# Decode attention: scores by row matmuls at tile positions, transposed back into the softmax layout, with two more key tiles on PE

## The chip, the cores and the metric

The kernel runs on one core of one Trainium2 chip. The metric is the device time of one launch in microseconds (us). Ratios are the mean time of one kernel's fast runs over that of the other's in the same rounds, so they are not quite the ratios of the medians quoted beside them.

Engines in the profile: PE is the matmul engine, PEld its weight loads, DVE is VectorE, ACT is ScalarE, SPq is the queue of SyncE, which issues the loads.

## The reference

Two independent attention blocks, A and B, one decode step each. Both have batch 8, 32 heads, 4096 cached keys of 128 elements, in bf16. The output is the two results side by side.

```python
def block(x, k_cache, v_cache, wq, wo):          # x [8,1,1024]; caches [8,32,4096,128]
    q = (x @ wq) -> [8, 32, 1, 128]
    scores = einsum("bhqd,bhkd->bhqk", q, k_cache) * 128 ** -0.5
    p = softmax(scores, axis=-1)
    o = einsum("bhqk,bhkd->bhqd", p, v_cache)
    return o.reshape(8, 1, 4096) @ wo
```

There is one query per batch and head, so every cached element is used once. The caches are 1074 of the 1107 MB that are read.

## The kernel before

A *unit* is one (block, head, batch) triple: 1 MB of K and 1 MB of V. There are 512 units, in groups of four. K arrives with 32 tiles of 128x128 per unit (partition = key, free = element). The scores of a unit are made by two engines:

- PE takes the first 12 tiles (`PEJOBS = (4, 2)` counts pairs). It transposes pairs as f32, ACT copies the result to `kt`, and each transposed tile becomes the *stationary* operand of a matmul with the query as a narrow moving operand. The scores land directly in the layout `S` (partition = key).
- VectorE takes the other 20 tiles with one multiply-and-accumulate call (a *dot*) per tile. The trace shows each dot as two instructions, SCALAR_TENSOR_TENSOR and DVE_READ_ACCUMULATOR (10240 of each), so one dot less per unit is 1024 instructions less.

```python
PEJOBS = (4, 2)                       # NPT = 12 tiles on PE, ND = 20 on VectorE
NK = 5; NV = 6                        # slots for K and V loads

def make_SC(q):                       # scores on PE, column layout
    for il in range(PEJOBS[c]):
        for e in range(2):
            pe.matmul(grp[:, gb, col:col + NMOV],                 # NMOV = 32
                      kt[:, ktslot, i * 256 + e:(i + 1) * 256:2], # stationary: 128x128
                      qm[:, blk, qo:qo + NMOV], start=(e == 0), stop=(e == 1))

def make_dots(U):                     # scores on VectorE, one call per tile
    for t in range(ND):
        v.scalar_tensor_tensor(out=junk[:, n % JR, :], in0=knat[:, slot, j*128:(j+1)*128],
            scalar=1.0, in1=qbc_sb[:, U % NQB, :], op0=ALU.mult, op1=ALU.mult,
            accum_out=S_all[:, r, gi * NT + j:gi * NT + j + 1])

def sp_k(U):                          # a K slot is reused when PE and VectorE are done with it
    deps = [("Tpe", Up * NC + NC - 1), ("dot", Up, ND - 1)]       # Up = U - NK
    sp.dma_start(knat[:, slot, :], K[b, h])                       # 128 rows of 8 KB
# ... softmax chain per group, PV matmuls, output projection: not touched in what matters here
```

Of the kernel before, what the change touches and what calls it, by code (L numbers as in the profile page):

```python
# [12 lines left out]
G = 4  # L13
# [5 lines left out]
NR = 3  # L19
NGB = 2  # L20
NOB = 2
NO = 2
NWO = 4
QHJ = 4
NMOV = 32
PEJOBS = (4, 2)
NQB = 8
# [21 lines left out]
def bass_concat_heads__mha_block_cached__mha_block_cached__decode_kernel(  # L49
# [42 lines left out]
    assert H % QHE == 0 and QHE * 128 <= 512  # L92
    NQJ = H // QHE
    PVD = G + 2 + (int(DOTLAG + 0.999) if NDC > 0 else 0)
    DV = PVD - 2
    NV8 = NT // 4
    assert LAG < 4 and NT % 4 == 0 and G == 4
    assert G * NPT + NMOV <= 192 and NMOV <= 64

# [3 lines left out]
    L_OFF = 328  # L103
    QW = 4 * UPB + NMOV

# [7 lines left out]
    with ExitStack() as es:  # L113
# [6 lines left out]
        kt = sb("kt", [128, NKT, NPT * 128], BF16)  # L120
        wq_sb = sb("wq_sb", [128, DC, H * 128], BF16)
        wo_sb = sb("wo_sb", [128, NWO, DO], BF16)
# [8 lines left out]
        junk = sb("junk", [128, JR, 128], BF16)  # L131
        S_all = sb("S_all", [128, NR, G * NT], F32)
        qm = sb("qm", [128, NBLK, QW], BF16)
        P_sb = sb("P_sb", [128, NR, G * NT], BF16)
# [13 lines left out]

        stage = ps("stage", [128, 4, 512], F32)
        grp = ps("grp", [128, NGB, 512], F32)  # L150
# [5 lines left out]
        sem_names += ["xd%d" % i for i in range(NBLK)]  # L156
        sem_names += ["wqd%d" % i for i in range(NBLK)] + ["wqd0a"]
        sem_names += ["kd%d" % i for i in range(NK)]
# [33 lines left out]
        def new_job(pe_ev, ev_ev):  # L192
            jid = len(jobs)
            jobs.append((pe_ev, ev_ev))
            deps = [jobs[jid - 4][1]] if jid >= 4 else []
            return jid % 4, deps

# [25 lines left out]
        def make_Q1(qj):  # L223
            blk, jl = qj // NQJ, qj % NQJ
            h0 = jl * QHE
            pe_ev, ev_ev = ("Q1pe", qj), ("Q1ev", qj)
            bank, sdeps = new_job(pe_ev, ev_ev)

            def emit_pe(pe):
                last = None  # L230
                for c in range(DC):
                    last = pe.matmul(stage[0:Bsz, bank, 0:QHE * 128],  # L232
                                     xT_sb[:, blk, c, :],
                                     wq_sb[:, c, h0 * 128:(h0 + QHE) * 128],
                                     start=(c == 0), stop=(c == DC - 1))
                return last
            wdep = ("wqd0a",) if qj == 0 else ("wqd", blk)
            pe_add(_Op("Q1_%d" % qj, "pe", emit_pe, deps=[wdep, ("Xev", blk)] + sdeps,
                       event=pe_ev, sem="pe_stA"))

            def emit_ev(a):
                return a.copy(qrow[0:Bsz, qj % 3, :], stage[0:Bsz, bank, 0:QHE * 128])
            d2 = [pe_ev]
            if qj >= 3:
                d2.append(("Q2pe", qj - 3))
                pj = qj - 3
                ulast = (pj // NQJ) * UPB + ((pj % NQJ) + 1) * QHE * Bsz - 1
                if ND > 0:
                    d2.append(("QBpe", ulast))
            add(_Op("Q1ev%d" % qj, "act", emit_ev, deps=d2, event=ev_ev, sem="ev_A"))  # L250
# [80 lines left out]
        def make_T(q):  # L331
# [24 lines left out]
            if U - NKT >= 0:  # L356
                d2.append(("SC", (U - NKT) * NC + c))
            if use_act:
# [3 lines left out]

        def make_SC(q):
            U, c = q // NC, q % NC
            blk, h, b = unit_info(U)
            ul = U % UPB
            g = U // G
            gi = U % G
            gb = g % NGB
            ktslot = U % NKT  # L370

            def emit_pe(pe):
                last = None
                for il in range(PEJOBS[c]):
                    i = POFF[c] + il
                    col = S_OFF + gi * NPT + 2 * i
                    for e in range(2):
                        qo = (ul * 2 + e) * 2
                        last = pe.matmul(grp[:, gb, col:col + NMOV],  # L379
                                         kt[:, ktslot, i * 256 + e:(i + 1) * 256:2],  # L380
                                         qm[:, blk, qo:qo + NMOV],
                                         start=(e == 0), stop=(e == 1))
                return last
            deps = [("Tev", q)]
            if gi == 0 and c == 0 and g - NGB >= 0:
                deps.append(("rl", g - NGB))
            if c == 0:
                hl = min(H - 1, (ul * 4 + 2 + NMOV - 1) // (4 * Bsz))
                deps.append(("Q2ev", blk * NQJ + h // QHE))
                deps.append(("Q2ev", blk * NQJ + hl // QHE))  # L390
                deps.append("qmz")
            pe_add(_Op("SC%d" % q, "pe", emit_pe, deps=deps, event=("SC", q), sem="pe_sc"))

        def make_chain_T1(g):
            gb, r = g % NGB, g % NR
            pe_add(_Op("T1_%d" % g, "pe",
                       lambda pe: pe.transpose(grp[0:G, gb, T1_OFF:T1_OFF + 128], pmax[:, r, :], ident_f[:, :]),  # L397
                       deps=[("rmax", g)], event=("T1", g), sem="pe_misc"))

# [114 lines left out]
        def make_chain_rest(g):  # L514
            gb, r, ob = g % NGB, g % NR, g % NOB
            lastq = (g * G + G - 1) * NC + NC - 1
            s_view = S_all[:, r, :]
            d0 = [("SC", lastq)]
            if g - NR >= 0:
                d0.append(("xs", g - NR))  # L520
            add(_Op("copyS%d" % g, "dve",
                    lambda v: v.tensor_copy(  # L522
                        S_all[:, r, :].rearrange("p (g j) -> p g j", g=G)[:, :, 0:NPT],
                        grp[:, gb, S_OFF:S_OFF + G * NPT].rearrange("p (g j) -> p g j", g=G)),
                    deps=d0, event=("copyS", g), sem="dve_misc"))
            d1 = [("copyS", g)]
            if ND > 0:
# [41 lines left out]

        add(_Op("o4z", "dve", lambda v: v.memset(o4[:, :, :], 0.0), event="o4z", sem="dve_misc"))  # L570

        def make_fin(blk):
# [12 lines left out]
        for g in range(NG):  # L585
            ulast = g * G + G - 1
            u_sc = ulast + (NC - 1 + LAG + 1) / float(NC)
            u_dots = ulast + 1 + DOTLAG if ND > 0 else 0.0
            u0 = max(u_sc, u_dots)
# [25 lines left out]
        for hh in range(NHH):  # L615
# [3 lines left out]
            if hh % H == H - 1:  # L619
                at_tick(t + 2, "F", hh // H)  # L620
        last_tick = max(extras.keys())
        order_rank = {"Q1": 0, "Q2": 1, "QB": 2, "T1": 3, "B": 4, "L": 5, "PV": 6, "O": 7, "OP": 8, "F": 9}
        makers = {"T1": make_chain_T1, "B": make_chain_B, "L": make_chain_L, "PV": make_PV,
                  "O": make_O, "Q1": make_Q1, "Q2": make_Q2, "OP": make_OP, "F": make_F, "QB": make_QB}

# [4 lines left out]
        for t in range(0, max(last_tick, NQCH + LAG) + 1):  # L630
            if t < NQCH:
                make_T(t)
            if 0 <= t - LAG < NQCH:
                make_SC(t - LAG)
            for kind, arg in sorted(extras.get(t, []), key=lambda ka: (order_rank[ka[0]], ka[1])):
# [16 lines left out]

        def sp_wq(blk):
            if blk == 0:
                def emit_a(sp):
                    src = blocks[0][3].rearrange("(p c) n -> p c n", c=DC)[:, :, 0:QHE * 128]
                    return sp.dma_start(wq_sb[:, :, 0:QHE * 128], src)
                add(_Op("wq0a", "sp", emit_a, deps=[], event=("wqd0a",), sem="wqd0a", amount=16))
                return

            def emit(sp):
                src = blocks[blk][3].rearrange("(p c) n -> p (c n)", c=DC)
                return sp.dma_start(wq_sb[:, :, :].rearrange("p c n -> p (c n)"), src)
            deps = [("Q1pe", blk * NQJ - 1)]
            add(_Op("wq%d" % blk, "sp", emit, deps=deps, event=("wqd", blk), sem="wqd%d" % blk, amount=16))

        def sp_wq0b():
            def emit_b(sp):
                src = blocks[0][3].rearrange("(p c) n -> p c n", c=DC)[:, :, QHE * 128:H * 128]
                return sp.dma_start(wq_sb[:, :, QHE * 128:H * 128], src)  # L670
            add(_Op("wq0b", "sp", emit_b, deps=[], event=("wqd", 0), sem="wqd0", amount=16))

# [38 lines left out]
        for i in range(NU + DV + 1):  # L711
            if i < NU:
                if i == 2 and NQJ > 1:
                    sp_wq0b()
                for blk in range(1, NBLK):
                    if i == max(3, min(blk * UPB - 40, (blk - 1) * UPB + (NQJ - 1) * QHE * Bsz - 24 + 6)):
                        sp_wq(blk)
                if i % Bsz == 2:
                    sp_wo(i // Bsz)
                sp_k(i)  # L720
# [149 lines left out]
```

## Time and profile before

The median is 2823.28 us over 12 runs (2819.29 to 2825.72).

| | before |
|---|---|
| DMA | 1111 MB, mean 394 GB/s |
| VectorE busy | 2425 us (86%) |
| PE busy | 2185 us (77%) |
| ACT busy | 675 us (24%) |

From the page of the kernel before: the span, the engines' busy time (and number of instructions), the rate in 40 equal slices, and the DMA queues (packets, MB, share of 16 engines' span).

```profile
span 2820.1 us, 60232 instructions
...
PE 2184.9 (77%) x15904; PEld 1214.3 (43%) x15904; DVE 2425.7 (86%) x21829; ACT 675.2 (24%) x1843; POOL 4.9 (0%) x11
...
GB/s 392 420 411 394 394 400 394 395 396 403 401 385 399 398 387 419 394 392 391 398 404 394 387 400 391 396 393 398 396 401 392 397 399 396 396 402 389 396 399 272
DMA packets 159302, 1111.27 MB, mean 394 GB/s; under 512 B 17488, under 2 KB 18512, under 8 KB 27760
...
q1 hardware_dynamic: 158928, 1107.40, 97.7%
q8 instruction: 127, 2.08, 0.3%
q14 instruction: 215, 1.76, 0.2%
...
```

The DMA engines look full (97.7%), but they don't run at one rate: one slice shows 420 GB/s, most show 390 to 400. The windows view of the kernel before (the last three columns are granted PE clock, DMA share, GB/s) shows it more sharply:

```profile
core 0: us, PE busy (x) PEld busy (x) DVE busy (x) ACT busy (x) POOL busy (x), PEclk, DMA share, GB/s
126.00:132.00 6.00, 3.60 (x29) 1.84 (x27) 5.90 (x55) 1.03 (x3) 0.00 (x0) 1.00 1.02 419
1524.00:1530.00 6.00, 4.34 (x41) 2.40 (x39) 5.56 (x52) 1.61 (x6) 0.00 (x0) 1.00 0.95 345
1554.00:1560.00 6.00, 4.14 (x34) 2.27 (x31) 5.93 (x54) 1.04 (x3) 0.00 (x0) 1.00 0.95 356
...
```

Early in the run the rate is 419 GB/s with VectorE 98% busy; later, with VectorE 93 to 99% busy, it falls to 345 and 356 in places. The waits of the load queue, and PE's waits for K (the columns after the colon are us in total, times, longest):

```profile
...
SPq L813 <- DVE junk L322: 2178.7, 507, 16.9
SPq L704 <- PE o L424: 118.0, 103, 6.6
...
```

```profile
...
PE stage L342 <- DMA knat<-in_A_k_cache_dram: 264.3, 154, 20.8
...
PE stage L342 <- DMA knat<-in_B_k_cache_dram: 241.7, 157, 3.2
...
```

It would be natural to read the first of these lines as "VectorE is the bottleneck": 2179 us long the queue waited for a dot to free a K slot. But PE waits 506 us for K, and a K load, once issued, takes 15.4 us to land, six times the 2.6 us that one MB needs at 400 GB/s. Loads are always queued. Something in the DMA, not the issue, is late.

The completion records of the trace tell what. Each load adds 16 to its semaphore. The Trainium skill, "DMA: Bandwidth & Descriptors", § Why a DMA increments its semaphore by 16 and not by 1, says that a DMA "runs on up to 16 SDMA engines that finish independently", each adding one; the trace agrees in that 16 separate increments are recorded for each load. Below are the times of the 16 increments of five K loads, in us after the first of them (computed from the trace's records, not a view of the profile):

```
unit  10:   0.0   0.0   0.1   0.1   0.2   0.2   0.5   1.0   1.5   1.7   1.9   2.0   2.3   2.9   3.0   3.7
unit  20:   0.0   0.0   0.0   0.1   0.1   0.2   1.0   1.1   1.5   1.9   2.0   2.9   3.0   3.3   3.8   6.7
unit  30:   0.0   0.1   0.2   0.2   0.7   1.0   1.1   1.6   1.9   2.0   2.9   3.0   3.0   3.3   3.8  10.5
unit 100:   0.0   0.0   0.0   0.1   0.1   0.1   0.2   0.3   0.3   0.4   0.5   0.8   1.4   1.6   2.8  10.1
unit 300:   0.0   0.2   0.2   0.4   0.4   0.5   0.5   0.5   0.6   0.6   1.0   1.1   1.2   1.3   2.0   9.6
```

One engine falls behind in the first 200 us until it is about 10 us late. There the five K slots stop the others: the first increment of a K load comes a median 5.4 us after its issue, the last 15.4 us. The fifteen are soon done with what is queued, the late one never is. It alone sets the pace from then on.

Two more things from the packet records: K loads land 4.97 us apart in the median where no packet of queue 14 ran in between, and 5.93 us apart where one did; and 187 of the 221 such packets of 8 KB are followed, 0.31 us after their start, by a data packet of 8 KB that took far longer than the usual 309 ns (over 600), in the median 968. After an instant picked at random one finds such a packet in 4% of cases. (The 221 are those of the whole record, the page's 215 those of the span; the times below are from the start of the record, 10.8 us before that of the span.)

```
queue 14 packet at 309.71 us took 333 ns; data packet started 0.32 us after it took 968 ns
queue 14 packet at 327.10 us took 326 ns; data packet started 0.31 us after it took 968 ns
queue 14 packet at 341.29 us took 309 ns; data packet started 0.31 us after it took 839 ns
```

So such a packet costs its engine 0.31 us for itself and 0.968 - 0.309 = 0.66 us by the stretched packet, together 0.97 us. Queues 8 and 14 are of the kind "instruction": 2.08 + 1.76 MB are 64 bytes for each of the 60232 instructions. Queue 8's size fits PE's stream; queue 14's fits the rest, of which VectorE has 22475 instructions (those of the page plus its separate semaphore waits), or 176 packets of 8 KB.

Two groups and a piece of the timeline, for what the change touches. A group's columns are busy us, mean ns of one, idle before; a timeline row is start, us, instruction, count.

```profile
L322 DVE SCALAR_TENSOR_TENSOR junk<-knat,qbc_sb 128x128 bf16<-128x128 bf16 x10240 | 2237.8, 284 | 23.1 <-ACT qbc_sb L299 12.3
...
L322 DVE DVE_READ_ACCUMULATOR junk<-knat,qbc_sb 128x1 f32 x10240 | 826.6, 81 | 0.0
...
L379 PE MATMUL grp<-qm,kt 128*128 128x32 bf16 x6144 | 323.4, 180 | 0.0
...
```

```profile
...
1588.55 0.26 PE L379 MATMUL grp<-qm,kt 128*128 128x32 bf16 x4
1588.74 0.22 PE L291 MATMUL stage<-qrow,sel 8*128 8x128 bf16 x1
1588.89 0.44 PE L342 MATMUL stage<-ident_f,knat 128*128 128x128 f32 x2
1589.17 0.36 PE L379 MATMUL grp<-qm,kt 128*128 128x32 bf16 x8
1589.45 1.89 PE L424 MATMUL o<-vnat,P_sb 128*4 128x512 bf16 x8
...
```

The dots repeat every 0.213 us in the median (from the records). The 12 score matmuls of a unit take 0.19 us plus 0.28 us between the starts of their neighbours. That is 0.47 us per unit.

### The profile page before, as it was taken

To read this page: it belongs to the slowest core of one execution; us is meant where nothing else is said; L and a number is where in the kernel's file an instruction comes from. 1 tells how busy PE (TensorE), PEld (TensorE's weight loads), DVE (VectorE), ACT (ScalarE), POOL (GpSimd) and SP (SyncE) were. 2 spreads that over 40 slices of the span, in tenths; PEclk is the share of its full clock that TensorE was granted. 3 is DMA by queue.
4 is the path that set the end of the run, shared out by engine and by line. 5 is a ranking of instruction groups with operands and counts; after the bars stand their busy time and mean duration, and the time that the engine had idled before them with its cause. 6 is when DMAs were issued, how large, how long until landed. Compare 5 with 4: busy or idle time off the path is not lost.

```text
span 2820.1 us, 60232 instructions
## 1 busy us (share of the span) xinstructions
PE 2184.9 (77%) x15904; PEld 1214.3 (43%) x15904; DVE 2425.7 (86%) x21829; ACT 675.2 (24%) x1843; POOL 4.9 (0%) x11
## 2 busy tenths in 40 slices
PE   5787777778777887678887777877887787787777
PEld 3444444444444444344444444444444444444444
DVE  6888888888888889688888888888888888888886
ACT  2222222222222222122222222222222222222222
POOL 0000000000000000000000000000000000000000
PEclk7888898898988988788898898888888888888888
DMA  9999999999999999999999999999999999999996
GB/s 392 420 411 394 394 400 394 395 396 403 401 385 399 398 387 419 394 392 391 398 404 394 387 400 391 396 393 398 396 401 392 397 399 396 396 402 389 396 399 272
DMA packets 159302, 1111.27 MB, mean 394 GB/s; under 512 B 17488, under 2 KB 18512, under 8 KB 27760
## 3 DMA queue, kind: packets, MB, share of 16 engines
q1 hardware_dynamic: 158928, 1107.40, 97.7%
q8 instruction: 127, 2.08, 0.3%
q14 instruction: 215, 1.76, 0.2%
q10 hardware_dynamic: 32, 0.03, 0.0%
HBM read 1107.33 MB, written 0.03 MB: 393 GB/s over the span
## 4 chain that ended last, share of the span: by engine, by line
DMA 57%; DVE 27%; PE 14%; issue 1%; SPq 0%; ACT 0%; DVEq 0%
DMA knat<-in_B_k_cache_dram 29%; DMA knat<-in_A_k_cache_dram 28%; DVE junk L322 24%; PE o L424 7%; PE stage L342 4%; DVE pmax L530 1%; PE grp L379 1%; PE stage L446 1%; DVE S_all L522 1%; PE grp L403 1%; DVE dg L538 0%; DVE gmax L534 0%; PE stage L232 0%; PE stage L291 0%; PE grp L410 0%
## 5 line engine op out<-in xcount | busy, mean ns | idle before, releaser
L322 DVE SCALAR_TENSOR_TENSOR junk<-knat,qbc_sb 128x128 bf16<-128x128 bf16 x10240 | 2237.8, 284 | 23.1 <-ACT qbc_sb L299 12.3
L424 PE MATMUL o<-vnat,P_sb 128*4 128x512 bf16 x4096 | 1197.2, 446 | 0.0
L342 PE MATMUL stage<-ident_f,knat 128*128 128x128 f32 x3072 | 604.5, 311 | 508.7 <-DMA knat<-in_A_k_cache_dram 264.3
L359 ACT COPY kt<-stage 128x512 f32<-128x512 f32 (+1 forms) x1024 | 495.3, 484 | 1583.5 <-PE stage L342 1578.0
L322 DVE DVE_READ_ACCUMULATOR junk<-knat,qbc_sb 128x1 f32 x10240 | 826.6, 81 | 0.0
L342 PEld LDWEIGHTS stage<-ident_f,knat 128*128 128x128 f32 x3072 | 363.6, 153 | 774.6 <-issue 747.6
L424 PEld LDWEIGHTS o<-vnat,P_sb 128*4 128x4 bf16 x4096 | 342.3, 93 | 558.7 <-issue 259.6
L379 PEld LDWEIGHTS grp<-qm,kt 128*128 128x128 bf16 x6144 | 325.1, 101 | 21.2 <-issue 0.4
L379 PE MATMUL grp<-qm,kt 128*128 128x32 bf16 x6144 | 323.4, 180 | 0.0
L403 PE MATMUL grp<-dg,ones_f 4*128 4x4 f32 x256 | 63.5, 316 | 109.2 <-DVE dg L538 108.6
L454 DVE TENSOR_REDUCE oun<-stage 128x4 f32<-128x16 f32 x128 | 22.4, 175 | 139.6 <-PE stage L446 139.5
L299 ACT CAST qbc_sb<-stage 128x128 bf16<-128x128 f32 x512 | 138.6, 271 | 0.0
L554 ACT ACTIVATE P_sb<-xs_sb 128x128 bf16<-128x128 f32 x128 | 39.6, 309 | 370.7 <-DVE xs_sb L546 370.7
L522 DVE COPY S_all<-grp 128x48 f32<-128x48 f32 x128 | 26.5, 207 | 109.4 <-PE grp L379 109.3
L291 PE MATMUL stage<-qrow,sel 8*128 8x128 bf16 x512 | 119.5, 234 | 0.0
L567 ACT COPY osb<-o 128x512 f32<-128x512 f32 x128 | 74.6, 583 | 151.6 <-PE o L424 151.6
L403 PEld LDWEIGHTS grp<-dg,ones_f 4*128 4x128 f32 x256 | 52.2, 253 | 122.1 <-DVE dg L538 120.3
L446 PE MATMUL stage<-ident_f,osb 128*128 128x128 f32 x512 | 84.4, 288 | 0.7 <-ACT osb L567 0.7
L557 DVE TENSOR_REDUCE l_p<-P_sb 128x4 f32<-128x128 bf16 x128 | 36.6, 286 | 49.8 <-ACT P_sb L554 49.8
L446 PEld LDWEIGHTS stage<-ident_f,osb 128*128 128x128 f32 x512 | 53.9, 141 | 57.9 <-issue 56.8
L534 DVE TENSOR_REDUCE gmax<-grp 4x1 f32<-4x128 f32 x128 | 35.2, 275 | 28.1 <-PE grp L397 27.7
L291 PEld LDWEIGHTS stage<-qrow,sel 8*128 8x128 bf16 x512 | 46.9, 92 | 22.6 <-issue 6.7
(40 smaller groups left out, 441.9 us busy)
## 6 DMA issues: line engine op xcount, KB each, us to landing
knat<-in_A_k_cache_dram SPq DMA_DIRECT2D x256, 1024.0 KB, 15.4
vnat<-in_A_v_cache_dram SPq DMA_DIRECT2D x256, 1024.0 KB, 17.6
knat<-in_B_k_cache_dram SPq DMA_DIRECT2D x256, 1024.0 KB, 15.4
vnat<-in_B_v_cache_dram SPq DMA_DIRECT2D x256, 1024.0 KB, 17.6
wo_sb<-in_A_wo_dram SPq DMA_DIRECT2D x32, 256.0 KB, 18.1
wo_sb<-in_B_wo_dram SPq DMA_DIRECT2D x32, 256.0 KB, 18.1
wq_sb<-in_A_wq_dram SPq DMA_DIRECT2D x1, 7168.0 KB, 28.8
wq_sb<-in_A_wq_dram SPq DMA_DIRECT2D x1, 1024.0 KB, 8.3
```

The source lines that it names most:

```text
L291: return pe.matmul(stage[:, bank, 0:128], sel[0:Bsz, b, :], qrow[0:Bsz, qj % 3, hl * 128:(hl + 1) * 128], start=True, stop=True)
L299: add(_Op("QBev%d" % U, "act", lambda a: a.copy(qbc_sb[:, U % NQB, :], stage[:, bank, 0:128]), deps=d2, event=ev_ev, sem="ev_A"))
L322: return v.scalar_tensor_tensor(out=junk[:, n % JR, :], in0=knat[:, slot, j * 128:(j + 1) * 128], scalar=1.0, in1=qbc_sb[:, U % NQB, :], o ...
L342: last = pe.transpose(stage[:, bank, il * 128:(il + 1) * 128], knat[:, slot, i * 256:(i + 1) * 256].bitcast(F32), ident_f[:, :])
L359: add(_Op("Tev%d" % q, "act", lambda a: a.copy(dst, src), deps=d2, event=ev_ev, sem="ev_A"))
L379: last = pe.matmul(grp[:, gb, col:col + NMOV], kt[:, ktslot, i * 256 + e:(i + 1) * 256:2], qm[:, blk, qo:qo + NMOV], start=(e == 0), stop= ...
L403: lambda pe: pe.matmul(grp[:, gb, B_OFF:B_OFF + G], ones_f[0:G, :], dg[0:G, r, :], start=True, stop=True),
L424: last = pe.matmul(o4[32 * gi:32 * gi + 4, ob, 0:512], P_sb[:, r, gi * NT + 4 * g8:gi * NT + 4 * g8 + 4], vnat[:, slot, g8 * 512:(g8 + 1) ...
L446: last = pe.transpose(stage[:, bank, m * 128:(m + 1) * 128], osb[:, ob, m * 128:(m + 1) * 128], ident_f[:, :])
L522: lambda v: v.tensor_copy(S_all[:, r, :].rearrange("p (g j) -> p g j", g=G)[:, :, 0:NPT], grp[:, gb, S_OFF:S_OFF + G * NPT].rearrange("p ( ...
L554: lambda a: a.activation(out=P_sb[:, r, :], in_=xs_sb[:, r, :], func=ACT_FN.Exp),
L567: lambda a: a.copy(osb[:, ob, :], o4[:, ob, :]),
```

## The change

Scores on PE are turned round: the query (two columns) is the stationary operand, and up to 512 columns of the transposed keys stream past it. Each unit of a group writes its two rows at its own tile position (partitions 0, 32, 64, 96). ACT copies the rows of a group to SBUF, PE transposes them back, and VectorE writes them into `S`. This needs fewer PE instructions and leaves PE room for one more pair of tiles, so VectorE has 18 dots instead of 20 per unit. PSUM is made free by one `grp` bank and one staging bank less, SBUF by loading `wq` in halves.

```diff
-NGB = 2
+NGB = 1
-NMOV = 32
-PEJOBS = (4, 2)
+NSB = 3
+PEJOBS = (4, 3)
 ...
-        wq_sb = sb("wq_sb", [128, DC, H * 128], BF16)
+        wq_sb = sb("wq_sb", [128, DC, HPW * 128], BF16)        # half of the heads at a time
+        srows_sb = sb("srows_sb", [128, 2, 1024], F32)
-        stage = ps("stage", [128, 4, 512], F32)
+        stage = ps("stage", [128, NSB, 512], F32)
+        rows = ps("rows", [128, 2, 512], F32)
 ...
-        def make_SC(q):            # (shown above)
+        def make_SCM(U):
+                for rb, (p0, npair) in enumerate(((0, RB0), (RB0, RB1))):
+                    for e in range(2):
+                        mov = kt[:, ktslot, p0 * 256:(p0 + npair) * 256].rearrange(
+                            "p (i x e) -> p i x e", i=npair, e=2)[:, :, :, e]
+                        last = pe.matmul(rows[32 * gi:32 * gi + 2, rb, 0:npair * 128],
+                                         qm[:, blk, qo:qo + 2], mov,
+                                         start=(e == 0), stop=(e == 1),
+                                         tile_position=(0, 32 * gi))
+        def make_ST(gk):           # transposes back, then VectorE into S_all
+                for il in range(npair):
+                    last = pe.transpose(stage[:, bank, il * 128:(il + 1) * 128],
+                                        srows_sb[:, g % 2, (p0 + il) * 128:(p0 + il + 1) * 128],
+                                        ident_f[:, :])
+                return v.tensor_copy(dst, src)
 ...
-            add(_Op("copyS%d" % g, "dve", ... S_all <- grp ...))
+            add(_Op("srev%d" % g, "act", ... srows_sb <- rows ...))
```

## The prediction

> **What bounds the kernel.** DMA part of the page: 1111.27 MB at a mean of 394 GB/s, yet 6 us stretches (windows view) reach 420 to 425. The trace's completion records show why. Every 1 MB load increments its semaphore 16 times, once per DMA engine. After the first 200 us, fifteen increments come close together, the sixteenth about 10 us later (median spread 9.9). K loads land a median 15.6 us after issue, their first increment after only 4.9: fifteen engines run dry, one never does. K landings are 4.96 us apart (16 packets of 8 KB at 309 ns), or about 5.95 us in every third unit; the extra 1 us falls where a queue-14 packet of 8 KB runs. Queues 8 and 14 are "instruction": 2.08 + 1.76 MB = 64 bytes x 60232 instructions. VectorE has 22475 of them, about 176 packets, one per three units. (The Trainium skill, "Runtime: NRT & Kernel Launch", Instruction fetch mechanics, calls refills mostly hidden; this trace disagrees: each delays its engine about 1 us.) Sum for that engine: 512 x 4.95 + wo 45 + wq 37 + 170 x 0.97 = 2780 us, plus start and tail of about 12 us each, near the 2820 us span. VectorE (86% busy) and PE (77%) keep up; PE waits 506 us in total for K (waits view).
>
> **What the change does.**
> - VectorE: dots per unit 20 to 18, each 0.212 us, so -217 us; the copy of S (128 x 207 ns) becomes 256 evictions (+20 us). Busy near 2230 us. Instructions about 20550, 161 packets.
> - PE: 6144 score matmuls of 32 columns (0.47 us per unit) become 2048 of 512 or 384 columns: an estimated 0.8 us per unit from the 0.225 us repeat of the 512-column PV matmuls (1.5 us if the strided operand costs double); a seventh key transpose (+0.11), seven transposes per group of four (+0.25 per unit). From about 3.7 to 4.4 us of a 5.4 us unit; about 5400 instructions fewer.
> - ACT: bigger second kt copy, one 128x896 copy per group: 675 to about 850 us, off the path.
> - wq in 3 and 4 KB rows instead of 7 and 64 KB: +1 us per engine.
> - Group chain one unit longer, one grp bank, three staging banks: hidden, since the slow engine always has about five loads queued. At the tail +2 us.
>
> **How much counts.** Only VectorE's instruction packets: 15 x 0.97 = -14 us, +1, +2. The 200 us of VectorE work taken away are off the bound.
>
> **Prediction: 2810 us, range 2792 to 2835.** Faster by over 2%: 0.03; within 2%: 0.91; slower by over 2%: 0.06.
>
> **What would show it.** Right: one of 16 increments still about 10 us late; K intervals still 4.96 or about 5.95 us, the long ones a little rarer; queue 14 about 1.63 MB, queue 8 about 1.74; VectorE near 79% busy, its idle time grown by what its work shrank; about 396 GB/s. Wrong: the spread shrinks well under 10 us, so an engine, most likely PE, holds issues back; then PE's waits for K shrink toward zero and waits on the ACT row copy or the staging banks grow.
>
> **What would make it wrong.** Strided 512-column reads at half rate plus drains between tile positions, putting PE above 5.4 us per unit; a staging bank waiting for VectorE's in-order queue; or the lag being due to something other than instruction packets, so that relieving VectorE pays more.

## The result and the profile after

The change is slightly faster: a median of 2803.22 us over 10 runs (2801.73 to 2808.02) against 2823.28 us. The ratio is 0.993 (95% interval 0.9921 to 0.994), or about 20 us.

The page of the changed kernel, the same lines as above:

```profile
span 2801.4 us, 52449 instructions
...
PE 2345.9 (84%) x13216; PEld 1148.2 (41%) x13216; DVE 2242.4 (80%) x19910; ACT 904.6 (32%) x1971; POOL 4.8 (0%) x11
...
GB/s 389 420 405 407 397 395 395 394 411 399 400 400 395 399 403 395 402 400 404 397 392 401 399 403 394 391 412 402 397 401 384 406 407 389 396 401 406 397 388 285
DMA packets 162238, 1110.77 MB, mean 397 GB/s; under 512 B 17520, under 2 KB 18544, under 8 KB 30864
...
q8 instruction: 106, 1.74, 0.2%
q14 instruction: 196, 1.61, 0.1%
...
```

VectorE has 183 us less to do (2425 to 2242 us), and the span fell by 19 us. PE has 17% fewer matmuls but is busier. The rate is 397 GB/s for 394. Queue 14 carries 196 packets for 215, queue 8 carries 106 for 127.

The groups, and PE's timeline:

```profile
L330 DVE SCALAR_TENSOR_TENSOR junk<-knat,qbc_sb 128x128 bf16<-128x128 bf16 x9216 | 2018.1, 285 | 16.7 <-ACT qbc_sb L307 13.0
...
L387 PE MATMUL rows<-kt,qm 128*2 128x512 bf16 (+1 forms) x2048 | 537.7, 388 | 0.0
...
L418 DVE COPY S_all<-stage 128x32 f32<-128x32 f32 (+1 forms) x256 | 47.4, 185 | 181.4 <-PE stage L407 181.4
...
L551 ACT COPY srows_sb<-rows 128x896 f32<-128x896 f32 x128 | 115.9, 905 | 40.8 <-PE rows L387 40.8
...
```

```profile
...
1512.15 0.95 PE L387 MATMUL rows<-kt,qm 128*2 128x512 bf16 x4
1513.04 0.23 PE L299 MATMUL stage<-qrow,sel 8*128 8x128 bf16 x1
...
1513.67 1.89 PE L454 MATMUL o<-vnat,P_sb 128*4 128x512 bf16 x8
...
```

The four score matmuls of a unit now take 0.89 us from their start to that of the next instruction, for 0.47 before. The strided moving operand did not halve the rate: 448 columns on average in about 0.22 us each, much like the 512-column PV matmuls (eight in 1.8 us). The copy of rows on ACT takes 905 ns a group.

The waits of the load queue, and those of the engines that bear on it:

```profile
...
SPq L847 <- DVE junk L330: 1699.1, 426, 7.6
SPq L737 <- PE o L454: 541.8, 150, 13.8
...
```

```profile
...
PE stage L350 <- DMA knat<-in_A_k_cache_dram: 203.2, 144, 12.7
...
PE stage L350 <- DMA knat<-in_B_k_cache_dram: 191.1, 150, 12.7
...
DVE S_all L418 <- PE stage L407: 181.4, 116, 4.1
...
```

The queue waits less for dots and more for PV matmuls, VectorE waits 181 us for the transposes back, PE still waits 394 us for K. VectorE's idle time (span less busy) grew from 394 to 559 us, that is, by 165 of the 183 us that were taken from it. In the completion records the sixteenth increment is still a median 9.0 us later than the first (9.9 before). K loads still land 4.97 or 5.93 us apart; the intervals over 5.3 us became fewer, 203 for 222. Nineteen times 0.97 us is 18 us, near the 18.7 us between the spans. (65 of these long intervals before and 67 after hold a load of `wo` or `wq`; without an instruction packet an interval with a `wo` load takes 5.6 us in the median.)

### The profile page after: what moved, and what is told of

Read it like the earlier page. It is cut to its first block, busy times and chain, and to the rows that moved or that the text cites. A ratio compares the mean times of both kernels' runs of the same rounds, so it can differ in the third digit from the quotient of the medians.

```text
span 2801.4 us, 52449 instructions
## 1 busy us (share of the span) xinstructions
PE 2345.9 (84%) x13216; PEld 1148.2 (41%) x13216; DVE 2242.4 (80%) x19910; ACT 904.6 (32%) x1971; POOL 4.8 (0%) x11
## 3 DMA queue, kind: packets, MB, share of 16 engines
q8 instruction: 106, 1.74, 0.2%
q14 instruction: 196, 1.61, 0.1%
## 4 chain that ended last, share of the span: by engine, by line
DMA 59%; PE 25%; DVE 13%; issue 1%; ACT 1%; SPq 1%; DVEq 0%
DMA knat<-in_A_k_cache_dram 31%; DMA knat<-in_B_k_cache_dram 28%; DVE junk L330 11%; PE o L454 8%; PE rows L387 7%; PE stage L350 6%; PE stage L407 2%; PE stage L299 1%; PE stage L240 1%; PE grp L440 0%; ACT P_sb L583 0%; DVE xs_sb L575 0%; DVE gmax L563 0%; DVE l_p L586 0%; DVE dg L567 0%
## 5 line engine op out<-in xcount | busy, mean ns | idle before, releaser
L330 DVE SCALAR_TENSOR_TENSOR junk<-knat,qbc_sb 128x128 bf16<-128x128 bf16 x9216 | 2018.1, 285 | 16.7 <-ACT qbc_sb L307 13.0
L367 ACT COPY kt<-stage 128x512 f32<-128x512 f32 (+1 forms) x1024 | 547.0, 534 | 1248.8 <-PE stage L350 1247.5
L454 PE MATMUL o<-vnat,P_sb 128*4 128x512 bf16 x4096 | 868.8, 391 | 0.0
L330 DVE DVE_READ_ACCUMULATOR junk<-knat,qbc_sb 128x1 f32 x9216 | 751.3, 82 | 0.1
L387 PE MATMUL rows<-kt,qm 128*2 128x512 bf16 (+1 forms) x2048 | 537.7, 388 | 0.0
L454 PEld LDWEIGHTS o<-vnat,P_sb 128*4 128x4 bf16 x4096 | 280.6, 86 | 441.0 <-issue 96.1
L387 PEld LDWEIGHTS rows<-kt,qm 128*2 128x2 bf16 x2048 | 133.8, 84 | 260.1 <-issue 135.9
L407 PE MATMUL stage<-ident_f,srows_sb 128*128 128x128 f32 x896 | 140.7, 303 | 0.0
L551 ACT COPY srows_sb<-rows 128x896 f32<-128x896 f32 x128 | 115.9, 905 | 40.8 <-PE rows L387 40.8
L407 PEld LDWEIGHTS stage<-ident_f,srows_sb 128*128 128x128 f32 x896 | 107.9, 153 | 9.9 <-issue 0.4
```

The costliest lines, as they stand in the source:

```text
L330: return v.scalar_tensor_tensor(out=junk[:, n % JR, :], in0=knat[:, slot, j * 128:(j + 1) * 128], scalar=1.0, in1=qbc_sb[:, U % NQB, :], o ...
L367: add(_Op("Tev%d" % q, "act", lambda a: a.copy(dst, src), deps=d2, event=ev_ev, sem="ev_A"))
L387: last = pe.matmul(rows[32 * gi:32 * gi + 2, rb, 0:npair * 128], qm[:, blk, qo:qo + 2], mov, start=(e == 0), stop=(e == 1), tile_position= ...
L407: last = pe.transpose(stage[:, bank, il * 128:(il + 1) * 128], srows_sb[:, g % 2, (p0 + il) * 128:(p0 + il + 1) * 128], ident_f[:, :])
L454: last = pe.matmul(o4[32 * gi:32 * gi + 4, ob, 0:512], P_sb[:, r, gi * NT + 4 * g8:gi * NT + 4 * g8 + 4], vnat[:, slot, g8 * 512:(g8 + 1) ...
L551: lambda a: a.copy(srows_sb[:, g % 2, 0:NPP * 128], rows[:, :, :].rearrange("p b x -> p (b x)")[:, 0:NPP * 128]),
```

## The experiments

Theory A: the DMA engine that also reads VectorE's instructions sets the pace, and the time follows the number of VectorE instructions. Theory B: VectorE's time counts, because a dot frees the K slot. Theory C: all instruction bytes count, or, what the change seems to be about, PE's shorter stream. A further rival is that the row layout paid, not the two dots.

The eleven kernels of the experiments all gave a correct result. Instructions are counted in the trace, with separate semaphore waits; queue 8 packets are those of the page or the trace. The labels are explained below.

| kernel | VectorE instr. | VectorE busy us | queue 8 packets | median us |
|---|---|---|---|---|
| before | 22475 | 2425 | 127 | 2823.28 |
| after | 20429 | 2242 | 106 | 2803.22 |
| a_vpad12 | 26146 | 2246 | 106 | 2848.97 |
| a_vlong | 20557 | 2408 | 106 | 2805.85 |
| a_ppad | 20429 | 2242 | 112 | 2802.97 |
| a_ppad2 | 20429 | 2242 | 138 | 2801.19 |
| b_43 | 20427 | 2229 | 139 | 2806.31 |
| a_42 | 22477 | 2465 | 101 | 2823.36 |
| m_43 | 5069 | 2374 | 106 | 2686.03 |
| m_44 | 4045 | 2073 | 111 | 2676.10 |
| m_44_d1 | 3021 | 2014 | 111 | 2672.86 |
| m_44_ppad2 | 4045 | 2076 | 143 | 2677.58 |
| b_m44 | 4043 | 2088 | 151 | 2678.13 |

A straight line through these thirteen medians, over the number of VectorE instructions divided by 128 (64 bytes into 8 KB), has a slope of 0.99 us and misses none by more than 3.6 us. Through the eight kernels with more than 20000 VectorE instructions alone the slope is 1.04 us. Neither of the two columns after it sorts the times. Nor does the granted PE clock, which is 0.855 in the profile of the kernel before and 0.928 after: it is 0.903 in a_42, which is no faster than the kernel before, and 0.929 in a_vpad12, the slowest of all.

### More VectorE instructions without work

```diff
 def emit(v, ...):                       # dots of the changed kernel
+    if t < 12:
+        v.wait_ge(sems["pool_misc"], 1) # has long passed
     return v.scalar_tensor_tensor(...)
```

> The changed kernel with 12 more VectorE instructions per unit (6144 in all), each a wait for a semaphore that has long passed: no data, hardly any time. Theory A (the DMA engine that also fetches VectorE's instructions sets the pace): 48 more queue-14 packets of 8 KB, each delaying that engine 0.97 us, so about +46 us, near 2850 us, with the late sixteenth increment still about 9 us behind. Theory B (VectorE's time sets when K slots come free, so its work counts): only what 12 idle instructions take, so near 2803 us, or a rise that comes with VectorE gaps and a spread that shrinks. Theory C (all instruction bytes count alike, whichever engine): also a rise, but see the PE run.

Measured: 2848.97 us, ratio to before 1.0085 (1.0069 to 1.0102). From the page:

```profile
span 2845.5 us, 58166 instructions
...
PE 2344.2 (82%) x13216; PEld 1147.3 (40%) x13216; DVE 2245.9 (79%) x19910; ACT 905.4 (32%) x1971; POOL 4.8 (0%) x11
...
q14 instruction: 240, 1.97, 0.2%
...
```

The trace holds 5717 more VectorE instructions, not 6144 (some waits were merged), or 44.7 packets; 45.8 us over the changed kernel is 1.02 us for each. VectorE's busy time did not change, its dots repeat every 0.213 us in both kernels, and the spread of the increments is 9.6 us, so the loads were as plentiful as before. Theory A named 2850 us.

### VectorE work without instructions

```diff
+                if gi == 0 and t == 9:   # once per group of four units
+                    v.memset(pad_sb[:, :], 0.0)      # 128x1640 f32
```

> The changed kernel with one memset of 128x1640 f32 on VectorE per group of four units, about 1.7 us each, which gives back the 217 us of VectorE time that the change took away but only 128 instructions (one packet). Theory A: 2803 to 2806 us. Theory B: back to about 2820 us or more.

Measured: 2805.85 us, ratio to before 0.9931 (0.9916 to 0.9946), not to be told from the changed kernel's own 0.993.

```profile
span 2804.3 us, 52577 instructions
...
PE 2362.3 (84%) x13216; PEld 1159.0 (41%) x13216; DVE 2408.1 (86%) x20038; ACT 905.1 (32%) x1971; POOL 4.8 (0%) x11
...
q14 instruction: 197, 1.61, 0.1%
...
```

The memset took 1.43 us, not 1.7, so 166 of the 183 us came back (2408 us busy). With VectorE nearly as busy as before the change, the time is within 3 us of the changed kernel's. This is against theory B.

### More PE instructions

Two attempts. In the first, extra waits were put before the PV matmuls:

```diff
                 for g8 in range(NV8):
+                    for _ in range(2 if g8 < 3 else 1):
+                        pe.wait_ge(sems["pool_misc"], 1)
                     last = pe.matmul(o4[...], ...)
```

> The changed kernel with 11 more PE instructions per unit (5632), again waits for a semaphore long passed: PE's stream is back at the size it had before the change, 22 more packets of 16 KB on queue 8. Theory A: these are fetched by another DMA engine, which has slack: 2803 to 2806 us. Theory C: 22 packets of 16 KB cost as much as or more than 22 of 8 KB: at least +20 us, 2823 us or more.

Measured: 2802.97 us, ratio 0.9921 (0.9906 to 0.9936). But only 1536 instructions were added, 6 packets, since most of the waits were merged; the test was weak. It was done again with tiny matmuls, all 8192 instructions of which are in the trace:

```diff
                 last = None
+                for _ in range(4):       # twice per unit
+                    pe.matmul(stage[0:4, bank, 0:4], ident_bf[:, 0:4], ident_bf[:, 0:4], start=True, stop=True)
                 for il in range(PEJOBS[c]):
                     last = pe.transpose(stage[:, bank, ...], ...)
```

> The changed kernel with 8 tiny PE matmuls (4 columns, 4 rows) more per unit, written into the staging bank of the key transposes before these overwrite it: 8192 more PE instructions, 32 more packets of 16 KB on queue 8 (the earlier PE run added only 1536, most of its waits having been merged). Theory A: 2803 to 2806 us. Theory C (instruction bytes count whichever engine reads them): at least +31 us, 2834 us or more.

Measured: 2801.19 us, ratio 0.9915 (0.9898 to 0.9931).

```profile
span 2799.1 us, 60641 instructions
...
q8 instruction: 138, 2.26, 0.3%
q14 instruction: 196, 1.61, 0.1%
...
```

With 32 packets of 16 KB more on queue 8 the kernel is not slower. Theory C is out: PE's shorter stream, the visible saving of the row matmuls, is worth nothing here.

### The layout without the dots, and the dots without the layout

```diff
-PEJOBS = (4, 2)          # in the kernel before
+PEJOBS = (4, 3)
```

> The kernel before with only its key split changed from 12 to 14 tiles on PE, so 18 dots instead of 20 on VectorE, with the old score layout (column matmuls, no transposes back). Theory A: VectorE loses 2048 instructions, 16 packets, about -15 us: 2806 to 2809 us, so the row layout is not what paid. Rival (the row layout and PE's smaller stream paid): near 2822 us.

```diff
-PEJOBS = (4, 3)          # in the changed kernel
+PEJOBS = (4, 2)
```

> The changed kernel with the old key split: 12 tiles on PE, 20 dots on VectorE, the new row layout, the smaller PE stream, the smaller wq tile. Theory A: VectorE's stream is as long as before the change (22475 less a few waits plus 128), so 2815 to 2824 us: the layout alone pays at most the few us that the dots do not explain. Rival (layout and PE's stream paid): near 2803 us.

Measured: b_43 2806.31 us, ratio 0.9935 (0.992 to 0.995); a_42 2823.36 us, ratio 0.9995 (0.998 to 1.001). With the kernel before and the changed one this makes a square:

| median us | column matmuls | row matmuls |
|---|---|---|
| 20 dots | 2823.28 | 2823.36 |
| 18 dots | 2806.31 | 2803.22 |

The two dots pay 17 us in the old layout and 20 us in the new one. The layout pays nothing at 20 dots and 3 us at 18, which is of the size of the intervals. The gain came from the line `PEJOBS`, and the old layout could have had it.

### Fewer VectorE instructions for the same work

If theory A holds, the dots themselves should be merged: one product over several tiles with the query broadcast, then one reduction over the same tiles.

```diff
-            for t in range(ND):              # one call per tile
-                v.scalar_tensor_tensor(..., accum_out=S_all[...])
+            for p in range(DP):              # m_43: DP = 3, six tiles each
+                v.tensor_tensor(out=junk[... w tiles], in0=knat[... w tiles],
+                                in1=qbc_sb[...].unsqueeze(1).to_broadcast([128, w, 128]), op=ALU.mult)
+                v.tensor_reduce(out=S_all[... w columns], in_=junk[... w tiles], axis=AX.X, op=ALU.add)
```

The products are now rounded to bf16 before they are summed; the outputs were still judged correct.

> The changed kernel with the 18 dots of a unit done by 3 products over 6 tiles each and 3 reductions over 6 tiles each: 6 VectorE instructions per unit for 36, so about 5100 in all, 40 queue-14 packets for 160. Theory A: this engine is no longer the late one; the next is the one that fetches PE's stream (106 packets of 16 KB; while the lag built up in the run before, it fell back an estimated 0.6 us each), so the floor is near 2710 us. But VectorE handles 2 x 2304 elements per unit: [...] VectorE may bound it near 2750 us. Rival (VectorE's time counts, not its instructions): slower than 2803 us, since VectorE's work per unit does not fall.

> As m_43, with 16 key tiles on PE and 16 dots on VectorE in 2 products and 2 reductions of 8 tiles[...]. Theory A: near 2710 to 2730 us, and the spread between the first and the last of the 16 increments falls or follows queue 8's packets. Rival: near 2800 us.

Measured: m_43 2686.03 us, ratio 0.951 (0.9494 to 0.9526); m_44 2676.10 us, ratio 0.9477 (0.9463 to 0.9491). Both were faster than expected. From the page of m_44, with the two VectorE groups:

```profile
span 2674.3 us, 37345 instructions
...
PE 2357.0 (88%) x13856; PEld 1169.1 (44%) x13856; DVE 2073.3 (78%) x3526; ACT 970.9 (36%) x1971; POOL 4.8 (0%) x11
...
GB/s 388 420 420 420 420 420 419 420 417 420 420 419 419 420 419 417 415 420 420 420 414 420 420 418 419 409 419 420 416 420 414 420 420 419 420 416 418 417 415 308
...
q8 instruction: 111, 1.82, 0.3%
q14 instruction: 68, 0.56, 0.1%
...
L344 DVE TENSOR_REDUCE S_all<-junk 128x8 f32<-128x1024 bf16 x1024 | 1230.5, 1212 | 7.0
...
L330 DVE TENSOR_TENSOR junk<-knat,qbc_sb 128x1024 bf16<-128x1024 bf16 x1024 | 686.3, 680 | 14.7 <-ACT qbc_sb L308 11.9
...
```

The windows of m_44 at the times shown of the kernel before:

```profile
...
126.00:132.00 6.00, 5.20 (x31) 2.61 (x28) 3.57 (x11) 2.81 (x6) 0.00 (x0) 1.00 1.02 422
1524.00:1530.00 6.00, 5.38 (x29) 2.44 (x29) 5.97 (x8) 2.69 (x5) 0.00 (x0) 1.00 1.01 418
1554.00:1560.00 6.00, 4.76 (x29) 2.56 (x28) 3.94 (x10) 2.34 (x6) 0.00 (x0) 1.00 1.00 415
...
```

m_43 is the sharpest test: VectorE is nearly as busy as it was before the change (2374 against 2425 us), yet the kernel is 117 us faster than the changed one, 0.98 us for each of the 120 packets fewer. The rate is about 420 GB/s throughout. (The Trainium skill, "HBM Reference", § Specifications (TRN2), gives about 425 GB/s for a core that streams alone; the 415 to 422 of these windows come near it.) Two assumptions of the expectations failed. VectorE did not bound m_43: its 2374 us are 4.64 us per unit, less than the 4.97 us between K loads. And the floor of 2710 us assumed that PE's packets would set the pace next, at 0.6 us each; both kernels went below it.

The records of m_43 also let one see whose packets count. A queue-14 packet comes about every 128 instructions of VectorE, ScalarE and SyncE, so most packets can be put down to one of them by counting (computed from the trace's records, not a view of the profile). Taken without the first 40 K loads and without intervals that hold a load of `wo` or `wq`, the intervals between K landings are (in us):

| interval holds | before: number, median, over 5.3 | m_43: number, median, over 5.3 |
|---|---|---|
| no instruction packet | 199, 4.96, 9 | 282, 4.97, 0 |
| a packet of VectorE's | 138, 5.93, 125 | 34, 5.92, 29 |
| of queue 14's, one of ScalarE's alone | 14, 4.97, 4 | 17, 4.97, 1 |
| one of PE's alone | 53, 4.96, 5 | 67, 4.97, 1 |
| SyncE's, mixed or not assigned | 7, 5.08, 3 | 9, 4.96, 1 |

So the late engine is held back by VectorE's packets and, but for a few intervals, by neither ScalarE's nor PE's.

### Where the bound went

> m_44 with one product and one reduction of 16 tiles per unit: 1024 VectorE instructions fewer, 8 packets. If VectorE's fetch engine is still the late one in m_44: -8 us, near 2668 us. If another bounds it: 2674 to 2678 us.

> m_44 with the same 8192 PE instructions more. If in m_44 the engine that fetches PE's stream has become the late one, its 32 packets add 10 to 30 us to 2676 us; if the VectorE, ACT or plain DMA load still bounds it, it stays within 4 us, unless PE (88% busy, plus an estimated 0.3 us per unit) runs out of time, which would show as PE no longer waiting for K.

> The kernel before, with its old column score matmuls, 16 key tiles on PE and the merged dots of m_44. Theory A: the row layout is not needed for the gain: 2672 to 2684 us, the same as m_44. Rival (the row layout and PE's shorter stream matter once VectorE's stream is short): slower than m_44 by 15 us or more.

The first sets `DP = 1`, the second adds the tiny matmuls shown above to m_44, the third puts `PEJOBS = (4, 4)` and the merged dots into the kernel before, with its column matmuls.

Measured: m_44_d1 2672.86 us, ratio 0.946 (0.9446 to 0.9474); m_44_ppad2 2677.58 us, ratio 0.9478 (0.9464 to 0.9492); b_m44 2678.13 us, ratio 0.948 (0.9466 to 0.9494).

m_44_d1 won 3 us, between the 8 us and the nothing that were expected: VectorE's packets have almost stopped mattering. (By the count above, 1 of 16 intervals with a packet of VectorE's is over 5.3 us in m_44_d1 and none of 23 in b_m44, for 13 of 25 in m_44. Intervals with one of PE's alone now are at times: 10 of 80 and 18 of 100, against 2 of 282 and 9 of 259 with none.) In its completion records the median lag of the ninth increment rose to 4.0 us (0.4 in the changed kernel) and that of the sixteenth is 7.0 us, so there is no longer one late engine but a slope over all sixteen. What is left is near the loads themselves: an estimate of 512 x 4.97 us, 88 us for `wo` and `wq` (packet times over 16 engines in the changed kernel, which loads them alike) and 24 us of start and tail is 2657 us of the 2673.

PE's stream still costs nothing measurable (+1.5 us for 32 packets). And b_m44 is within 2 us of m_44, so the row layout is not needed for the best version either. m_44_d1 beats both kernels, the one before by 5.4% (ratio) and the changed one by 4.7% (medians of different rounds).

## Why the prediction was right

The predicted 2810 us, within 2%, and the range 2792 to 2835 us hold the measured 2803.22 us. That alone shows little: the range also holds the 2823 us of no change, and the predicted effect was 13 us of the measured 20. What bears the prediction out is its mechanism. Point by point:

- *"Fifteen engines run dry, one never does."* Held: the late increment stayed (9.9 to 9.0 us). With a seventh of VectorE's stream (m_44_d1) the fifteenth is nearly as late as the sixteenth, 6.6 against 7.0 us, and likewise in m_44_ppad2 and b_m44; in the changed kernel it was 1.8 against 9.0.
- *"Only VectorE's instruction packets"*, *"The 200 us of VectorE work taken away are off the bound"*. Shown from three sides: instructions without work cost 1.02 us a packet (a_vpad12), work without instructions cost nothing clear (a_vlong), the same work in fewer instructions gained 117 us (m_43). Of the 183 us, 165 became idle time. The "5.95 us in every third unit" was loose: 222 of 511 intervals are long, because those with a load of `wo` or `wq` are long too.
- *"-14 us, +1, +2"*, net -11 us. The effect was -20 us, so the sum was too small. The packets were 16 fewer rather than 15, and 0.99 us each by the line through all runs, so -16 us. The longer tail cost 0.8 us, not 2 (last V landing to last output: 11.4 and 12.2 us). The wq rows cost the engines 3.8 us on average, not 1 (packet times summed over 16 engines: 41.0 and 44.8 us). These make -11 again; some 9 us of the gain remain. The trace counts 19 long K intervals fewer, which covers the difference of the spans, but why it is 19 and not 16, and why the wq cost does not show, is not settled.
- *PE: "0.8 us" per unit for the score matmuls, not the 1.5 of a halved rate.* 0.89 us. PE's busy time rose by 161 us and it still waited 394 us for K.
- *Queue 14 about 1.63 MB, queue 8 about 1.74, VectorE near 79% busy, about 396 GB/s.* 1.61, 1.74, 80% and 397. *ACT about 850 us* was short: 905 us, of no consequence.
- The feared staging bank and the drains between tile positions did not show: PE's key transposes waited 1.1 us in all for VectorE's copies out of the staging banks, and their weight loads 1.9 us; the row matmuls of a unit took 0.89 us. A drain at a change of position was not measured by itself.

Left open: which of the sixteen engines is the late one, since the records don't name it. That VectorE's packets hold it back is seen in the K intervals above and in the experiments; that the same engine is the late one throughout is inferred from the lag that builds up. Open too is why PE's packets, twice as large, cost nothing. They are not free to the engine that carries them: in the kernel before, each took 0.99 us in the median and 119 of 127 were followed by a data packet of over 600 ns (median 800). Nor is it likely that they all lie on one engine with slack: in m_44_ppad2 143 packets at 1.08 us are 154 us, while an estimate of 2675 - 512 x 4.97 - 88 leaves an engine some 40 us. So they are spread over engines, or their time overlaps that of the data packets; no run tells which.

## What to carry to other kernels

When a streaming kernel looks DMA-bound below the rate it reaches in its own best stretch, look at the sixteen completion increments of one load before believing the waits of the issue queue: one late engine makes every slot look as if compute held it. Instructions are loads too; in this unrolled kernel, 128 VectorE instructions cost about 1 us of one DMA engine, so fewer and wider instructions can pay where less work doesn't. And when a change has two parts, try the small one alone: here one tuple gave 17 of the 20 us.

## What the Trainium skill lacked or had wrong

- "Runtime: NRT & Kernel Launch", § Instruction fetch mechanics, calls the cost of a refill "mostly hidden". Here each 8 KB refill of VectorE's stream cost the kernel 0.97 to 1.02 us, about 170 us of 2823. The page speaks of the engine that runs the instructions; what it leaves out is that the refill takes time from a DMA engine that the loads need.
- The same section gives refills of 16 KiB blocks. In these traces queue 8 has packets of 16384 bytes (127 before), but queue 14 has packets of 8192, one about every 128 instructions of VectorE.
- "DMA: Bandwidth & Descriptors", § Queues, rings and completion order, says that an engine alternates between its queues by packets; no page gives the price of the switch. The 8 KB data packet after an instruction packet mostly took 968 ns (queue 14) or 800 ns (queue 8) instead of 309.
- No page says that instruction refills can make one engine of the sixteen late and so hold a whole stream of loads back, or how to see it: the sixteenth increment 10 us late, with 0.5 us between the first and the ninth.
- No page says whether PE's refills cost a stream of loads anything. Here no cost was measured: 32 more packets of 16 KB changed the time by -2.0 us in one kernel and +1.5 us in another.
